# A new order of steps for an attention pair, with weight loads, x loads and one small addition moved

## The chip, the cores and the metric

The kernel runs on one core of a Trainium2 chip. The metric is the device time of one execution in microseconds. The engines meant below are TensorE (PE, with its weight loads PEld), VectorE (DVE), ScalarE (ACT), GpSimd (POOL) and SyncE (SP), whose queue issues nearly all transfers.

## The reference

Attention with a relative-position bias over 4 batches, 8 heads, 576 positions and head width 64, followed by a two-layer MLP with an ELU between its layers (2304 tokens, 512 to 2048 to 512):

```
scores = (q @ k.T) / 8 + bias          # bias: a small MLP of log1p(|i-j|) / log1p(i), per head
attn   = exp(scores - max); attn /= sum(attn) + 1e-9
x      = attn @ v, as 2304 x 512
h      = x @ w_in;  g = h if h > 0 else exp(h) - 1
out    = g @ w_out                     # the MLP's weights are given as float64
```

## The kernel before, in words

The program has three stages that follow each other: the bias is built (`bias_phase`), attention runs over 16 pairs of heads (`attention`), and the MLP (`mlp`) runs to the end. The order of instructions on every engine is that of the code; nothing reorders them.

**A pair.** Pair n (two heads of batch n // 4) has its scores in five groups: u = 0 to 3 are 128 query rows of both heads each, u = 4 holds the 64 rows that are left of both heads. A line of the table `STEPS` is one of the five steps 0 to 4 of an iteration; a token such as `aX20` has a prefix (`a`: the iteration's own pair n; `y`: the pair before it), a letter and numbers:

- `S u`: the score matmuls (`ps`, line 299). With u < 4 they fill two banks of PSUM, one for each head; there are two such buffers in all, so the next `S` waits until DVE has read them.
- `X u e`: `expo`. DVE adds the bias and takes the minimum (`ss<-ps,bias`, line 319), ACT takes exp (line 330), and after the second head GpSimd copies the last 64 columns to `md` (line 333).
- `T u`: PE transposes the result into two of three buffers `wt`; `P u r X` copies one of them to SBUF with engine A (ACT) or V (DVE). `M` and `Q` do the same for `md`; `M0a0` (`trans_spare`) uses spare columns of the score banks and needs two copies `Q`, `M0` (`trans_mid`) uses one of the three buffers and needs one.
- `V h j`: the matmuls with v (`wv`, line 426); half 0 takes u = 0, 1 and 4, half 1 takes u = 2 and 3. `C h X` copies a half out, from where SP stores it to `xd` in DRAM.

**The weights.** In iteration N the raw float64 weights of block f = N - 1 are turned into float32: `low` (GpSimd multiplies the upper words, line 273; DVE the lower words, line 277), `sign` (DVE, line 281; SP then issues the load of the next block's `raw`, which has a single buffer), `shift` (DVE, line 283, and then GpSimd's integer addition, line 286). SP stores the result to `wf` in iteration N + 1, after step 1.

**q and k.** `load_pair(n + 2)` issues five transfers; `high` (in step 2 of iteration N, DVE, line 118) and `rest` (in step 3, GpSimd, line 122: `kl`, `ql`, `qd`) split pair N + 1 into a high and a low part.

**x.** The table `early` gives a token (`one`, `two`) or the end of a step of iteration N something of the MLP's input: `load_x` (lines 466 and 470: 3 or 9 transfers of attention's output and of its reciprocal sums), `scale_x` (DVE multiplies them, line 478), `high_x` (line 501) and `low_x` (line 504).

**The sums.** After a batch's fourth pair `invert` adds 1e-9 (line 341) and takes the reciprocal (line 342), both by DVE, and `turn` transposes it for DRAM. After the last pair the lines of `LAST` are run, and then the MLP starts.

Of the kernel before, what the change touches and what calls it, by code (L numbers as in the profile page):

```python
# [24 lines left out]
def kernel(  # L25
# [68 lines left out]
    def load_pair(n):  # L94
        b, hp = pairs[n]
        kk, qq = st["kq", n] = [ld.tile([P, S], F32, tag=t, name=t, bufs=2) for t in ("kk", "qq")]

        nc.sync.dma_start(out=kk[0:D], in_=kT[b, hp, :, 0])
        nc.sync.dma_start(out=kk[D:P, 0:NCH * P], in_=kT[b, hp, :, 1, TAIL:])
        nc.sync.dma_start(out=kk[D:P, NCH * P:], in_=kT[b, hp, :, 1, 0:TAIL])  # L100
        for e in range(2):
            nc.sync.dma_start(out=qq[e * D:(e + 1) * D], in_=qT[b, hp, :, e])
# [21 lines left out]
    def load_v(n):  # L124
        b, hp = pairs[n]
        vv = st["v", n] = ld.tile([P, NU, D], F32, tag="vv", name="vv", bufs=2)
        nc.sync.dma_start(out=vv, in_=vt[b, hp])
# [210 lines left out]

    def invert(b):
        sm = st["sm", b].rearrange("p h u -> p (h u)")  # L340
        nc.vector.tensor_scalar(sm, sm, 1e-9, None, op0=ALU.add)
        nc.vector.reciprocal(sm, sm)

    def turn(b):
        sm = st.pop(("sm", b)).rearrange("p h u -> p (h u)")
# [182 lines left out]
    def attention():  # L528
# [6 lines left out]


        STEPS = (
# [5 lines left out]
        )  # L543
        LATE = (
# [5 lines left out]
        )  # L550
        LAST = (
            "yT3 yP30A yV00 yP31V yV01 yV02 yT2 yP20A yV03 yP21V yM0 yQ0V yM1 yQ1A",
            "yV04 yC0V yV10 yV11 yV12 yV13 yV14 yC1A",
        )
        late = []

        V, G = nc.vector, nc.gpsimd
        early = {
            (5, 1): [(load_x, 0, 0, 0)],
            (6, "one"): [(scale_x, 0, 0, 0, V)],  # L560
            (6, 1): [(load_x, 0, 1, 0)],
            (7, "one"): [(scale_x, 0, 1, 0, V)],
            (9, 1): [(load_x, 0, 0, 1)],
            (10, "one"): [(scale_x, 0, 0, 1, V)],
            (10, 1): [(load_x, 0, 1, 1)],
            (11, "one"): [(scale_x, 0, 1, 1, V)],
            (12, "two"): [(high_x, 0, "B11", xo["B11"], V.tensor_copy)],
            (13, "one"): [(low_x, 0, "B11", xo["B11"], V)],
            (13, "two"): [(high_x, 0, "B12", xo["B12"], V.tensor_copy)],
# [8 lines left out]
        def weights(f, op):  # L578
            if not 0 <= f < NFC:
                return  # L580
            if op == "low":
                decode(dp, f, "scale")
            decode(dp, f, op)
            if op == "sign" and f + 1 < NFC:
                decode(dp, f + 1, "load")
            if op == "shift":
                decode(dp, f, "add")
# [50 lines left out]
        def others(n, i):  # L638
            for fn, *args in early.get((n, i), ()):
                fn(*args)  # L640

        def aside(n, i):
            if i == 1:
                weights(n - 2, "store")
            if n == 0 and i == 2:
                split_high(1)
                split_low(1)
            if n > 0 and n % HP == 0:
                if i == 1:
                    invert(n // HP - 1)  # L650
                if i == 3:
                    late.extend(turn(n // HP - 1))
            others(n, i)
            if n < NP - 1:
                return
            if i == 0:
                load_w(0)
                load_w(1)
            if i == 2:
                high_w(0)  # L660
            if i == 3:
                low_w(0, nc.vector)
            if i == 4:
                load_w(2)
                high_w(1)

        for n in range(NP):
            for i, line in enumerate(STEPS if n < NP - 4 else LATE):
                flush()
                if i == 0:  # L670
                    if n + 2 < NP:
                        load_pair(n + 2)
                    load_v(n)
                step(n, line)
                aside(n, i)
        flush()
        weights(NP - 2, "store")
        weights(NP - 1, "low")
        weights(NP - 1, "sign")
        weights(NP - 1, "shift")  # L680
        invert(B - 1)
        others(NP, 0)
        step(NP, LAST[0])
        late += turn(B - 1)
        step(NP, LAST[1])
        weights(NP - 1, "store")
        others(NP, 1)
        low_w(1, nc.vector)
        flush()
        load_w(3)  # L690
        high_w(2)
# [351 lines left out]
```

## Time and profile before

| | us |
|---|---|
| median of 3 runs | 690.03 (688.99 to 690.52) |
| the profiled execution | 692.81 |
| its span, first to last instruction | 691.0 |
| PE, DVE, ACT, POOL busy in the span | 659.6, 483.8, 450.7, 133.7 |
| from the first score matmul of pair 0 to the MLP's first matmul | 56.4 to 306.9 |

The span is 1.8 us shorter than the profiled execution, and that execution is 2.8 us longer than the median of the runs. Times of rows count from the start of the span. The score matmuls of pair n's step 0 are where iteration n begins: pair 2 begins at 86.36 us, pair 15 at 283.63 us. PE's busy time is close to the whole span; its matmuls overlap, so the start of one instruction after another is the better measure of what they take.

### The profile page before, as it was taken

What the parts mean: (1) busy time and instruction counts of PE and PEld (TensorE: products, weight loads), DVE (VectorE), ACT (ScalarE), POOL (GpSimd) and SP (SyncE); (2) the same over time, 40 slices, a digit from 0 to 9 for tenths busy, and PEclk for the clock granted to TensorE, in tenths of its full rate; (3) what the DMA queues carried; (4) which work ended last, traced back from release to release, by engine and by line L of the source; (5) the groups of instructions that cost most, each with busy time, mean ns of one, the idle gap of its engine ahead of it and who ended that gap; (6) DMA issues with size and microseconds to landing.
All of it is one profiled execution on the core that took longest, in us unless ns stands there. A gap on an engine that the chain in (4) does not pass through costs nothing.

```text
span 691.0 us, 13847 instructions
## 1 busy us (share of the span) xinstructions
PE 659.6 (95%) x5246; PEld 528.1 (76%) x5246; DVE 483.8 (70%) x1003; ACT 450.7 (65%) x981; POOL 133.7 (19%) x168
## 2 busy tenths in 40 slices
PE   5997999979996999989999999999999999999997
PEld 3545667756675666769998898899899899899896
DVE  6997778858866798888777989745456754444443
ACT  6996789868885888967566666643444644344333
POOL 0002456545553555540000000000000000000000
PEclk9998899999998999999999999999999999999999
DMA  6999456776767556654678768998664465555202
GB/s 156 215 220 238 147 174 180 222 230 192 222 186 212 173 174 185 223 184 169 228 256 316 273 237 315 348 354 304 195 257 167 168 240 219 210 205 201 83 1 91
DMA packets 49938, 144.63 MB, mean 209 GB/s; under 512 B 13376, under 2 KB 26448, under 8 KB 42192
## 3 DMA queue, kind: packets, MB, share of 16 engines
q1 hardware_dynamic: 47840, 141.08, 63.0%
q10 hardware_dynamic: 2032, 2.67, 1.1%
q8 instruction: 41, 0.67, 0.4%
q14 instruction: 25, 0.20, 0.1%
HBM read 92.14 MB, written 40.97 MB: 193 GB/s over the span
## 4 chain that ended last, share of the span: by engine, by line
PE 72%; DMA 12%; ACT 8%; DVE 4%; issue 2%; SPq 1%; POOL 1%; DVEq 0%; ACTq 0%
PE acc L787 28%; PE h L836 26%; PE wv L426 7%; PE ps L299 6%; DMA raw<-in_wd_dram 4%; PE wt L384 3%; DMA wf<-da 3%; ACT bo L222 2%; ACT rel L199 2%; DMA bias<-bo 2%; DVE ss L319 2%; DMA rr<-rd 1%; ACT ss L330 1%; PE bps L209 1%; DMA T<-in_rtab_dram 1%
## 5 line engine op out<-in xcount | busy, mean ns | idle before, releaser
L787 PE MATMUL acc<-wB,gh 128*128 128x512 f32 x528 | 171.3, 392 | 0.0
L330 ACT ACTIVATE ss<-ss,nm 128x576 f32<-128x576 f32 x128 | 99.2, 778 | 26.7 <-DVE nm L319 26.3
L836 PE MATMUL h<-bias 128*128 128x384 f32 x552 | 111.4, 338 | 0.0
L787 PEld LDWEIGHTS acc<-wB,gh 128*128 128x128 f32 x528 | 98.1, 188 | 14.3
L319 DVE CUSTOM_DVE_ANT_0 ss<-ps,bias 128x576 f32<-128x576 f32 x128 | 91.6, 752 | 23.6 <-PE ps L299 12.1
L836 PEld LDWEIGHTS h<-bias 128*128 128x128 f32 x552 | 99.8, 188 | 7.5 <-DVE bias L504 0.4
L787 PE MATMUL acc<-wB,gl 128*128 128x512 f32 x264 | 103.8, 393 | 0.0
L816 ACT CAST gh<-e 128x384 fp32r<-128x384 f32 x96 | 49.4, 514 | 38.7 <-DVE e L815 37.7
L821 ACT ACTIVATE e<-c 128x384 f32<-128x384 f32 x66 | 34.6, 525 | 53.5 <-DVE c L867 53.4
L299 PE MATMUL ps<-kh,qh 64*128 64x288 f32 x256 | 52.2, 350 | 15.0 <-DVE nm L319 14.2
L810 DVE TENSOR_TENSOR gl<-e,gh 128x384 fp32r<-128x384 f32 x96 | 53.2, 554 | 18.9 <-ACT gh L816 16.4
L821 ACT ACTIVATE e<-h 128x384 f32<-128x384 f32 x28 | 13.8, 491 | 69.4 <-PE h L836 69.4
L815 DVE SCALAR_TENSOR_TENSOR e<-e,c 128x384 f32<-128x384 f32 x66 | 36.7, 557 | 30.6 <-ACT e L822 30.5
L299 PEld LDWEIGHTS ps<-kh,qh 64*128 64x128 f32 x256 | 29.8, 191 | 36.6 <-DVE nm L319 29.5
L836 PE MATMUL h<-bias,wA 128*128 128x384 f32 x276 | 56.3, 338 | 0.0
L426 PE MATMUL wv<-pta,vv 128*64 128x320 f32 (+1 forms) x320 | 55.6, 461 | 0.2 <-DVE pta L361 0.2
L209 PE MATMUL bps<-rel,cs 128*32 128x288 f32 x576 | 47.7, 424 | 8.2 <-ACT rel L199 7.8
L787 PEld LDWEIGHTS acc<-wB,gl 128*128 128x128 f32 x264 | 49.5, 187 | 7.8
L384 PEld LDWEIGHTS wt<-ident,ss 64*128 64x128 f32 x1024 | 44.6, 144 | 12.8 <-issue 6.2
L836 PEld LDWEIGHTS h<-bias,wA 128*128 128x128 f32 x276 | 50.2, 188 | 3.8
L384 PE MATMUL wt<-ident,ss 64*128 64x64 f32 x1024 | 50.0, 232 | 2.9 <-ACT ss L330 1.6
L822 ACT ACTIVATE e<-e 128x384 f32<-128x384 f32 x96 | 50.5, 526 | 3.0
(127 smaller groups left out, 1194.2 us busy)
## 6 DMA issues: line engine op xcount, KB each, us to landing
wB<-wB SPq DMA_DIRECT2D x22, 1024.0 KB, 5.0
raw<-in_wd_dram SPq DMA_DIRECT2D x16, 1024.0 KB, 6.9
bias<-wA SPq DMA_DIRECT2D x9, 1792.0 KB, 9.5
wA<-wA SPq DMA_DIRECT2D x8, 1792.0 KB, 12.0
wa<-wf SPq DMA_DIRECT2D x20, 512.0 KB, 5.0
bias<-bo SPq DMA_DIRECT2D x16, 576.0 KB, 8.4
wA<-bias SPq DMA_DIRECT2D x5, 1792.0 KB, 14.4
wf<-da SPq DMA_DIRECT2D x16, 512.0 KB, 8.2
```

The lines of the kernel that those rows point to most:

```text
L209: nc.tensor.matmul(ps[32 * g:32 * g + 32, f, 0:HS], lhsT=W2, rhs=rel[g][:, f * HS:(f + 1) * HS], start=True, stop=True,)
L299: nc.tensor.matmul(ps[:, f, 0:HS], lhsT=(qh, ql)[q][r, u * P:(u + 1) * P] if u < NCH else qd[n % 2][q], rhs=k[r, f * HS:(f + 1) * HS], sta ...
L319: nc.vector.tensor_tensor_reduce(out=s.rearrange("p (f x) -> p f x", f=2), in0=st["ps", n, u][e][:, :, 0:HS], in1=bap.rearrange("p (f x) - ...
L330: nc.scalar.activation(s, s, AF.Exp, bias=nm, scale=-1.0, accum_out=st["sm", b][:, hp, col:col + 1])
L384: nc.tensor.transpose(banks[r][:, x * TAIL:(x + 1) * TAIL], ss[q, c:c + P], ident[q, q])
L426: nc.tensor.matmul(st["pv", n, half][e * D:(e + 1) * D, 0:N], lhsT=l, rhs=r, start=start, stop=stop)
L787: nc.tensor.matmul(acc[j, t], lhsT=x[:, t * P:(t + 1) * P], rhs=w, start=(count[j, t] == 1), stop=(count[j, t] == 6 * NQ),)
L810: nc.vector.tensor_sub(gl, t, gh.bitcast(F32))
L816: nc.scalar.copy(g[i, e][0][:, h * HB:(h + 1) * HB], t)
L821: nc.scalar.activation(t, src, AF.Relu, scale=-1.0)
L822: nc.scalar.activation(t, t, AF.Exp, scale=-1.0)
L836: nc.tensor.matmul(ps, lhsT=a[f][c], rhs=x[y][c], start=(start and k == 0), stop=(stop and k == len(todo) - 1), skip_group_check=not start,)
```

## The change

`STEPS` and `LATE` (which have the same lines) get another order. `low` and `sign`, which stood on either side of `aX00` and `aX01`, follow each other on DVE; `shift` goes from step 1 to step 4. `trans_spare` is no longer used. The copies `P11` and `Q1` go from DVE to ACT, `C1` from ACT to DVE. `one` and `two` stand in step 3. `load_pair(n + 2)` is issued after step 2 and `load_v(n)` after step 0; both stood ahead of step 0. In `early` the loads of x get longer leads: from 1 to about 1.4 iterations for those of (5, 1) and (9, 1), and 2 iterations for the other two. The addition of 1e-9 becomes `lift` on GpSimd, after step 0; the reciprocal stays after step 1. `LAST` gets an order of its own, with the last block's weights inside.

```diff
     def invert(b):
         sm = st["sm", b].rearrange("p h u -> p (h u)")
-        nc.vector.tensor_scalar(sm, sm, 1e-9, None, op0=ALU.add)
         nc.vector.reciprocal(sm, sm)
+
+    def lift(b):
+        sm = st["sm", b].rearrange("p h u -> p (h u)")
+        nc.gpsimd.tensor_scalar(sm, sm, 1.0, 1e-9, op0=ALU.mult, op1=ALU.add)
...
         STEPS = (
-            "aS0 yM0a0 yT3 yQ01A yV02 one low aX00 yQ00A yP30A aX01 yV01 yV03",
...
+            "aS0 yT2 aX00 yP20A yP21A aX01 yV03 yV00 low",
+            "aS1 yT3 yV01 yP30A sign yV02 yM0 yP31A aX10",
+            "aS4 yQ0A aX11 yM1 yV04 yC0A yQ1A high aX40 aT0",
+            "aS2 two aP00A aP01A yV12 yV11 one yV14 aT4 rest aX20 aP40A aX21 aP41A",
+            "aS3 aT1 yV13 yV10 shift aP11A aP10A aX30 aX31 yC1V",
         )
...
         LAST = (
-            "yT3 yP30A yV00 yP31V yV01 yV02 yT2 yP20A yV03 yP21V yM0 yQ0V yM1 yQ1A",
-            "yV04 yC0V yV10 yV11 yV12 yV13 yV14 yC1A",
+            "yT2 yP20A yP21V yV00 yV01 low",
+            "yV02 yT3 yP30A yV03 yM0 yP31V yQ0V sign yM1 yQ1A",
+            "yV04 yC0V yV10 shift yV11 yV12 yV13 yV14 yC1A",
         )
...
             (5, 1): [(load_x, 0, 0, 0)],
-            (6, "one"): [(scale_x, 0, 0, 0, V)],
-            (6, 1): [(load_x, 0, 1, 0)],
-            (7, "one"): [(scale_x, 0, 1, 0, V)],
+            (6, "two"): [(scale_x, 0, 0, 0, V)],
+            (6, 3): [(load_x, 0, 1, 0)],
+            (8, "one"): [(scale_x, 0, 1, 0, V)],
             (9, 1): [(load_x, 0, 0, 1)],
-            (10, "one"): [(scale_x, 0, 0, 1, V)],
-            (10, 1): [(load_x, 0, 1, 1)],
-            (11, "one"): [(scale_x, 0, 1, 1, V)],
+            (10, "two"): [(scale_x, 0, 0, 1, V)],
+            (10, 3): [(load_x, 0, 1, 1)],
+            (12, "one"): [(scale_x, 0, 1, 1, V)],
...
         def aside(n, i):
             if i == 1:
                 weights(n - 2, "store")
+            if i == 0:
+                load_v(n)
+            if i == 2:
+                if n + 2 < NP:
+                    load_pair(n + 2)
...
             if n > 0 and n % HP == 0:
+                if i == 0:
+                    lift(n // HP - 1)
                 if i == 1:
                     invert(n // HP - 1)
...
                 flush()
-                if i == 0:
-                    if n + 2 < NP:
-                        load_pair(n + 2)
-                    load_v(n)
                 step(n, line)
                 aside(n, i)
         flush()
         weights(NP - 2, "store")
-        weights(NP - 1, "low")
-        weights(NP - 1, "sign")
-        weights(NP - 1, "shift")
+        lift(B - 1)
+        step(NP, LAST[0])
         invert(B - 1)
+        step(NP, LAST[1])
         others(NP, 0)
-        step(NP, LAST[0])
         late += turn(B - 1)
-        step(NP, LAST[1])
-        weights(NP - 1, "store")
+        step(NP, LAST[2])
         others(NP, 1)
         low_w(1, nc.vector)
+        weights(NP - 1, "store")
         flush()
```

Line numbers from 343 on are 3 higher in the changed kernel, and from 653 on a few more.

On SP, in iteration 9, where nine transfers for x are issued (`xr` and `rr`; `xd` and `wf` are stores), before:

```order
L439 DMA xd_75<-xs 128x256
L98 DMA kk<-in_k_dram 64x576
L99 DMA kk<-in_k_dram 64x512
L100 DMA kk<-in_k_dram 64x64
L102 DMA qq<-in_q_dram 64x576 x2
L127 DMA vv<-in_v_dram 128x576
L268 DMA raw<-in_wd_dram 128x2048
L288 DMA wf_89<-da 128x1024
L466 DMA xr_2302<-xd_74 128x2x128
L470 DMA rr<-rd_78 64x2x128 x2
L466 DMA xr_2302<-xd_74 128x2x64
```

and in the changed kernel:

```order
L442 DMA xd_75<-xs 128x256
L127 DMA vv<-in_v_dram 128x576
L268 DMA raw<-in_wd_dram 128x2048
L288 DMA wf_89<-da 128x1024
L469 DMA xr_2274<-xd_74 128x2x128
L473 DMA rr<-rd_78 64x2x128 x2
L469 DMA xr_2274<-xd_74 128x2x64
L473 DMA rr<-rd_78 64x2x64 x2
L469 DMA xr_2274<-xd_75 128x2x192
L473 DMA rr<-rd_79 64x2x192 x2
L98 DMA kk<-in_k_dram 64x576
```

The raw weights' load now has one transfer of v ahead of it in the iteration, not five of q and k as well; these come behind the loads of x.

On DVE, in steps 2 and 3 of iteration 13 (`high_x` is the cast of line 501 or 504, `low_x` the subtraction of line 504 or 507; the casts of line 118 are `high`), before:

```order
L319 ISA st_116,nm<-ps,biast 128x576
L319 ISA nm 128x1
L501 CAST bias<-xr_2302 128x768
L118 CAST qd_111<-qq 64x64 x2
L118 CAST qh<-qq 128x512
L118 CAST kh<-kk 128x576
L319 ISA ss,nm<-ps,bias 128x576
L319 ISA nm 128x1
L319 ISA ss,nm<-ps,bias 128x576
L319 ISA nm 128x1
L403 COPY pta<-wt 128x8x64
```

and in the changed kernel:

```order
L118 CAST qd_111<-qq 64x64 x2
L118 CAST qh<-qq 128x512
L118 CAST kh<-kk 128x576
L319 ISA st_116,nm<-ps,biast 128x576
L319 ISA nm 128x1
L504 CAST bias<-xr_2274 128x768
L507 TENSOR_TENSOR bias<-xr_2274,bias 128x768
L319 ISA ss,nm<-ps,bias 128x576
L319 ISA nm 128x1
L319 ISA ss,nm<-ps,bias 128x576
L319 ISA nm 128x1
L283 TENSOR_SCALAR da<-da 128x1024
```

`high` now stands ahead of `aX40`, and both operations on x stand between it and `aX20`, behind `high`, whose last cast lets GpSimd begin `rest`.

On GpSimd, around the change of batch after pair 11, in the changed kernel:

```order
L122 TENSOR_TENSOR kl<-kk,kh 128x576
L122 TENSOR_TENSOR ql<-qq,qh 128x512
L122 TENSOR_TENSOR qd_112<-qq,qd_111 64x64 x2
L333 TENSOR_SCALAR md<-ss 128x128
L286 TENSOR_TENSOR da<-da,dm 128x1024
L333 TENSOR_SCALAR md<-ss 128x128 x2
L273 TENSOR_SCALAR da<-raw 128x1024
L345 TENSOR_SCALAR sm<-sm 128x36
L333 TENSOR_SCALAR md<-ss 128x128
```

The addition of line 286 now stands between the copies `md` of u = 2 and u = 3, and line 345 is the new `lift`.

## Rows read from the trace of the kernel before

**Rows 1.** Busy time by stretch: PE, PEld, DVE, ACT, POOL, granted clock, DMA.

```profile
70.18:86.36 16.18, 16.09 (x174) 11.37 (x174) 11.72 (x30) 13.43 (x37) 7.97 (x10) 0.84 0.46 142
86.36:283.63 197.27, 184.37 (x2267) 129.49 (x2265) 154.51 (x370) 164.55 (x430) 107.33 (x130) 0.97 0.66 197
190.97:204.47 13.50, 13.50 (x177) 9.57 (x175) 10.91 (x27) 12.68 (x34) 7.96 (x10) 1.00 0.62 188
141.95:161.38 19.43, 15.42 (x176) 10.72 (x174) 11.77 (x28) 12.73 (x34) 7.88 (x10) 0.91 0.76 217
204.47:225.94 21.47, 16.21 (x176) 11.62 (x174) 11.86 (x28) 12.72 (x34) 7.95 (x10) 0.84 0.73 207
...
175.76:190.97 15.21, 14.55 (x178) 10.06 (x177) 12.92 (x31) 12.62 (x34) 8.21 (x10) 1.00 0.65 193
...
306.87:684.40 377.53, 377.53 (x1875) 340.44 (x1874) 237.45 (x420) 195.79 (x377) 1.37 (x1) 1.00 0.59 218
```

**Rows 2.** Timeline of DVE at the two long stalls: start, duration, idle before.

```profile
146.55 0.96 DVE L478 TENSOR_TENSOR xr<-xr,rr 128x768 f32<-128x768 f32 x1 [4.69 <-DMA rr<-rd]
...
210.31 0.96 DVE L478 TENSOR_TENSOR xr<-xr,rr 128x768 f32<-128x768 f32 x1 [5.93 <-DMA xd<-xs]
```

**Rows 3.** Waits: total us, times, longest.

```profile
DVE dm L277 <- DMA raw<-in_wd_dram: 5.3, 4, 2.0
```

**Rows 4.** Timeline of PE, steps 0 to 2 of pair 9.

```profile
190.97 0.40 PE L299 MATMUL ps<-kh,qh 64*128 64x288 f32 x2
...
191.86 0.28 PE L369 MATMUL ps<-ident,md 64*128 64x64 f32 x4
191.98 0.78 PE L384 MATMUL wt<-ident,ss 64*128 64x64 f32 x16
192.69 1.84 PE L426 MATMUL wv<-pta,vv 128*64 128x320 f32 x12
194.46 0.40 PE L299 MATMUL ps<-kh,qh 64*128 64x288 f32 x2
...
196.63 0.44 PE L358 MATMUL wm<-ident,md 128*128 128x128 f32 x2
```

**Rows 5.** Timeline of DVE after the scores of pair 9's step 0.

```profile
192.28 0.76 DVE L319 CUSTOM_DVE_ANT_0 ss<-ps,bias 128x576 f32<-128x576 f32 x1 [0.80 <-PE ps L369]
...
193.64 1.22 DVE L281 SCALAR_TENSOR_TENSOR dm<-raw,dm 128x1024 uint32<-128x1024 uint32 x1
```

**Rows 6.** Timeline of ACT: a copy `P` of pair 9.

```profile
195.25 0.58 ACT L403 COPY ptb<-wt 128x512 f32<-128x512 f32 x1
```

**Rows 7.** Timeline of DVE: the addition of 1e-9 twice, and `low_x` after the last pair.

```profile
120.24 1.22 DVE L341 TENSOR_SCALAR sm<-sm 128x36 f32<-128x36 f32 x1
...
301.42 0.18 DVE L341 TENSOR_SCALAR sm<-sm 128x36 f32<-128x36 f32 x1
...
304.94 1.60 DVE L504 TENSOR_TENSOR bias<-xr,bias 128x768 fp32r<-128x768 f32 x1
```

**Rows 8.** Timeline of POOL beside these, and `rest` of pair 8.

```profile
119.03 2.38 POOL L286 TENSOR_TENSOR da<-da,dm 128x1024 int32<-128x1024 int32 x1
...
186.53 1.42 POOL L122 TENSOR_TENSOR kl<-kk,kh 128x576 fp32r<-128x576 f32 x1 [1.85 <-DVE kh L118]
187.89 1.30 POOL L122 TENSOR_TENSOR ql<-qq,qh 128x512 fp32r<-128x512 f32 x1
...
303.90 1.82 POOL L492 TENSOR_TENSOR xr<-xr 128x768 f32<-128x768 f32 x1
```

**Rows 9.** Groups of DVE from 56 to 312 us: busy us, mean ns.

```profile
L501 DVE CAST bias<-xr 128x768 fp32r<-128x768 f32 x4 | 2.2, 554 | 0.0
```

**Rows 10.** Transfers of `raw`, us from issue to landing, all 16.

```profile
DMA to landing us min/median/max: 5.7/6.9/9.5
```

**Rows 11.** Timeline of SP: when pair 9's `raw` is issued.

```profile
197.88 0.36 SPq L268 DMA_DIRECT2D raw<-in_wd_dram  x1
```

**Rows 12.** Timeline of PE at the end of attention.

```profile
298.52 0.46 PE L384 MATMUL wt<-ident,ss 64*128 64x64 f32 x8 [1.29 <-ACT ss L330]
```

14 rows, old and new, of tables (LATE, STEPS) are left out of this document.

## The prediction

> **What bounds the kernel now.** I read the busy time by stretch first, then the timelines of the stretches that stand out. From 306.87 us on, PE is busy for the whole of 377.53 us at full clock [rows 1]: the MLP can only begin earlier or later. The change acts between 56 and 307 us, and the measure is the distance from one pair's first score matmul to the next one's.
>
> Pair 9 takes 13.50 us, and PE is busy in all of it [rows 1]: a pair without a wait. The 13 pairs 2 to 14 take 197.27 us, where 13 such pairs would take 13 x 13.50 = 175.5. So 21.8 us are waits. Pair 6 takes 19.43 and pair 10 takes 21.47 us, 5.9 and 8.0 too much, and both have one cause: DVE multiplies x as `one` in step 0, ahead of the pair's first `X`, and stood idle for 4.69 and 5.93 us until that transfer landed [rows 2]. PE, whose score banks DVE empties, stood behind it and was granted 0.91 and 0.84 of its clock over these pairs; pair 9 had all of it [rows 1]. Pair 8, in which a batch's sums are inverted, takes 15.21, 1.7 too much; pairs 4 and 12 are of its kind. DVE also waited for raw weights, 5.3 us in 4 pairs [rows 3].
>
> **PE's own work.** Nothing is removed from it. The spare-bank transposes `M0a0` become `M0`: 4 small matmuls that hold PE for 0.12 us (191.86 to 191.98) become two of the kind that lasts 0.44 and not 0.28 us [rows 4]; +0.1 a pair. The order moves PE's fill between scores. Step 0 had 3.49 us (190.97 to 194.46). Now it has scores 0.89, transposes 0.71 and two thirds of the value matmuls' 1.77, together 2.78 [rows 4]. DVE starts its first `X` 1.31 us after the scores begin and is through the second at 2.67, when `sign` starts [rows 4, 5]; with a tenth for the signal the next scores can start at about 2.8. PE and DVE are level there, where there was 0.7 us of slack, so I charge 0.15 a pair for jitter. `low` and `sign` then run beside the scores of step 1, whose fill has grown to 2.1 us. A pair without a wait: 13.50 + 0.1 + 0.15 = 13.75, x 13 = 178.8.
>
> ACT gains a copy of 0.58 us (`P11`) [rows 6] and `Q1` and loses `C1`, of like width; `Q0` becomes one copy from two. That adds 0.3 to 0.6 to the 12.68 of 13.50 us that it is busy [rows 1]: 13.0 to 13.3 of 13.75, and so still under PE.
>
> **Loads of x.** `scale_x` moves from step 0 to step 3, about 8 us later for the loads of (5, 1) and (9, 1); the waits were 4.69 and 5.93 us [rows 2]. The other two get over a pair more. I cost what remains at nothing. SP issues the nine transfers behind `raw`, and behind them stand only q and k, which DVE needs a pair later.
>
> **The small addition.** It took 1.22 us at 120.24 and 0.18 at 301.42, for the same 36 columns [rows 7]. The first ended at 121.46, just behind GpSimd's integer addition at 121.41 (119.03 + 2.38) [rows 8]: it was held until the other engine was done. On GpSimd it costs DVE nothing; the reciprocal stays. The transposition of the sums stays too, and the reciprocal now pushes `X11`, `high` and `X40`: I leave 0.5 in each of pairs 4, 8 and 12, 1.5 together.
>
> **What the new place of `one` and `two` costs.** The same hold works against the change. `high` now ends before `X40`, so GpSimd's `rest` begins while DVE is in `X40`: `kl` 1.42, `ql` 1.30 us [rows 8]. DVE then comes to a cast of 0.55 (`two`) [rows 9] and an operation of 0.96 (`one`) [rows 2], ahead of `X20`. Alone they take 1.5 us, and `X20` must wait as long anyway: 0.2 until its scores begin and 1.31 from there. Beside GpSimd they need not: after the last pair `low_x`, of the size of the 0.96, took 1.60 from 304.94 on, ending 0.82 behind GpSimd's subtraction at 305.72 (303.90 + 1.82) [rows 7, 8]. In pairs 12, 13 and 14 both stand there with `rest` (pair 15 has no `rest`; pairs 6, 8 and 10 have one operation). If `kl` comes first, DVE waits some 1.2 us for it, does the cast, waits 1.30 for `ql`, does the other: 4.0, which is 2.5 too late. If DVE's cast comes first, it waits for `kl` once: 0.55 + 1.42 + 0.96 = 2.9, or 1.4 too late. PE has about 0.15 of slack before step 3, so 1.25 to 2.35 in each of the three pairs. A single operation costs 0 to 0.6. Together 3.8 to 8.9; which comes first hangs on 0.2 us that my placing cannot resolve, so I take the middle, 6.3.
>
> The Trainium skill, page "SBUF — State Buffer", section "Who interferes with whom", says the same of the mechanism: GpSimd shares a port pair with VectorE, a VectorE instruction with two SBUF inputs or in a two-port mode competes for it, and the one that starts second "fully blocks". The 1.22 us bear that out. If it were a sharing by bandwidth instead, by the 1.60 against 0.96 us, the 1.5 us would become 2.5 and cost 0.85 in three pairs, 2.6 in all, and the time would be 3.7 lower than by the block.
>
> **Raw weights.** Landing took them 5.7 to 9.5 us [rows 10]. Their load waited on SP behind five transfers of q and k: pair 9's went out at 197.88 [rows 11], 3 us after `sign`, which ran from 193.64 for 1.22 [rows 5]. Now it goes out when `sign` and GpSimd's multiplication are done. The latter stands behind an `md` that needs ACT's exp, which I place 6 us into the pair. `low` wants the data 2.8 us into the next one, 10.5 us later. So the 5.3 us go.
>
> **Start and end.** Pair 1 (16.18 us at a granted clock of 0.84 [rows 1]) keeps its work and its cause, a pair 0 with no older pair to fill PE: 0, between -1.5 and +1.5. At the end PE waited 1.29 us for an exp [rows 12] and a little more behind it, since `T3` came first. Now `T2` does, whose exp is older. `Q0` on DVE gives back 0.3. I take -1.3, between -2 and 0. GpSimd's subtractions for the MLP now precede its last integer addition; their users come 4 us or more into the MLP.
>
> **The sum.** 178.8 + 1.5 + 6.3 = 186.6 against 197.3 is -10.7; with the end -12.0. From the profiled execution's 692.81 that is 680.8. The runs' median is 2.78 below that execution, which I carry over: 678.0 us.
>
> **Rivals.**
> 1. *The hold does not bite*, because GpSimd starts `rest` later than I place it, behind DVE's work on x. Then the 6.3 us vanish: 671.7. For it: `rest` also stands behind an `md` that waits for ACT. Against it: it began within 0.1 us of the last cast at 186.53 [rows 8].
> 2. *ACT becomes the bound.* Busy for 13.0 to 13.3 us, it also waits in each pair for a last value matmul before `C0` and for `T4` before `P40`, some 0.7 us as I place them. If these add up, a pair takes 14.0 to 14.2, about 0.35 more than 13.75: +4.5, so 682.5. Against it: it waited about 0.8 per pair before (13.50 - 12.68) and PE was full all the same [rows 1].
> 3. *Slower: GpSimd's integer addition catches `low`.* `shift` now sits in step 4, and the addition of 2.38 us [rows 8] behind it and behind an `md`. I place its end 1.6 us into the next pair, 1.2 us ahead of `low`. If ACT runs over 1.2 us later than I think, `low` is held as the small addition was, for up to 2.38, and `sign` and `X10` with it; 0.5 of that is slack. At 1.9 x 13 = 24.7 us the time is 702.7. It is slower than before once a pair loses 0.9 (12.0 / 13). Against it: ACT would have to fall that far behind in every pair.
> 4. *The change does not do what it says*: transfers queue as before and x or `raw` is waited for at the new places. Half of the 13.9 us of pairs 6 and 10 stays, 7.0: 685.0. Against it: 8 us of lead against waits of 5.93 at most.
>
> **Chances.** The forecast, 674 to 681.5: 0.52. Rival 1: 0.20. Rival 2: 0.13. Rival 4: 0.09. Rival 3: 0.06. The range 670.5 to 685.5 takes in the first four mostly and both ends of the hold's price. Anything within 0.2% of before (1.4 us, about what a measurement of this kernel can tell from no change) could only lie between rivals 3 and 4: faster 0.92, same 0.02, slower 0.06.
>
> **What would show it.** In the trace of the changed kernel: pairs 6 and 10 within 1 us of pair 9, and the multiplication of x with no idle time before it; no idle time before `low`; pairs 3, 5, 7, 9 and 11 at 13.6 to 13.9; pairs 12 to 14 at 15 to 16.5, with DVE's two operations between `X40` and `X20` longer than 0.55 and 0.96 and ending just behind a subtraction of GpSimd; the reciprocal without a long wait; `T2` at the end without idle time. I am wrong if ordinary pairs take over 14.2, or if pairs 12 to 14 look like pair 11.

## The result and the profile after

The changed kernel takes 679.0 us, the median of 4 runs (677.5 to 680.9), beside 690.0 us for the kernel before (689.0 to 690.5): a ratio of 0.984, with a 95% interval of 0.982 to 0.987. The forecast was 678.0. Its profiled execution took 678.97 us with a span of 677.1, where the one before had 692.81 and 691.0.

The forecast total was nearly met, but not by its own terms; in part that was luck. The busy time by stretch shows it; the columns are those of [rows 1]. The rows are, in order: pair 1; pairs 2 to 14; pair 9; pairs 4, 10, 12 and 13; pair 15 with the end of attention; the MLP.

```profile
69.93:85.54 15.61, 15.54 (x174) 10.95 (x172) 10.70 (x26) 13.53 (x35) 6.16 (x10) 0.86 0.45 136
85.54:268.82 183.28, 179.26 (x2241) 126.06 (x2239) 147.86 (x354) 167.93 (x431) 113.49 (x134) 1.00 0.72 211
183.56:197.12 13.56, 13.56 (x174) 9.58 (x172) 10.35 (x27) 12.55 (x34) 8.04 (x11) 1.00 0.60 178
112.64:127.75 15.11, 14.29 (x175) 9.93 (x173) 10.86 (x29) 13.37 (x35) 8.48 (x12) 1.00 0.71 210
197.12:211.88 14.76, 14.06 (x174) 9.89 (x172) 11.94 (x29) 13.11 (x35) 9.07 (x11) 1.00 0.83 248
225.36:241.81 16.45, 14.76 (x175) 10.11 (x174) 14.04 (x32) 13.02 (x35) 9.26 (x12) 1.00 0.74 239
241.81:255.26 13.45, 13.45 (x175) 9.49 (x173) 12.42 (x29) 12.79 (x34) 9.26 (x11) 1.00 0.58 175
268.82:290.82 22.00, 21.66 (x251) 13.81 (x249) 18.43 (x37) 18.02 (x44) 12.19 (x12) 1.00 0.64 204
290.82:677.10 386.28, 380.83 (x1886) 342.25 (x1884) 241.62 (x424) 197.47 (x380) 3.61 (x2) 1.00 0.59 219
```

Pairs 2 to 14 went from 197.27 [rows 1] to 183.28: -14.0, where -10.7 was forecast. Pair 15 and the end went from 23.24 to 22.00 (-1.2). What lies before pair 2 lost 0.8. The MLP, costed at nothing, went from 384.1 (306.87 to the end at 691.0) to 386.28: +2.15. Together that is -13.9, the difference of the spans. The long stalls of pairs 6 and 10 are gone, and with them the lowered clock: pairs 2 to 14 are granted 1.00, where [rows 1] had 0.97.

Three new waits stand in the trace. **The first** is in pairs 4, 8 and 12: the reciprocal waits 1.26 us for GpSimd's small addition. The timelines are POOL, then DVE, then PE, in pair 4; the columns are start, duration, the instruction, and in brackets the idle time before it and what ended it.

```profile
117.38 0.30 POOL L333 TENSOR_SCALAR md<-ss 128x128 f32<-128x128 f32 x1 [2.28 <-ACT ss L330]
117.64 1.18 POOL L273 TENSOR_SCALAR da<-raw 128x1024 f32<-128x1024 f32 x1
118.90 0.22 POOL L345 TENSOR_SCALAR sm<-sm 128x36 f32<-128x36 f32 x1
...
119.15 0.38 DVE L341 RECIPROCAL sm<-sm 128x36 f32<-128x36 f32 x1 [1.26 <-POOL sm L345]
119.45 0.70 DVE L319 CUSTOM_DVE_ANT_0 ss<-ps,bias 128x576 f32<-128x576 f32 x1
...
122.01 0.39 PE L299 MATMUL ps<-kh,qh 64*128 64x288 f32 x1 [0.82 <-DVE nm L319]
```

The addition itself is 0.22 us. But it is issued behind step 0, and so it stands in GpSimd's order behind an `md` that waits for ACT and behind the conversion of the raw weights. DVE, in its own order, has the reciprocal ahead of `X11`, and PE then waits 0.82 us for the score bank that `X11` should have emptied. Read such a wait from the queue of the engine that is named: the instruction named is short, what stands ahead of it is not.

**The second** is the hold between GpSimd and DVE, which was forecast for pairs 12 to 14. It is there in pair 12 and absent in pair 13. DVE and POOL, pair 12 and then pair 13:

```profile
234.61 1.36 DVE L504 CAST bias<-xr 128x768 fp32r<-128x768 f32 x1
235.89 2.02 DVE L481 TENSOR_TENSOR xr<-xr,rr 128x768 f32<-128x768 f32 x1
...
234.14 1.41 POOL L122 TENSOR_TENSOR kl<-kk,kh 128x576 fp32r<-128x576 f32 x1
235.52 1.58 POOL L122 TENSOR_TENSOR ql<-qq,qh 128x512 fp32r<-128x512 f32 x1
...
249.45 0.55 DVE L504 CAST bias<-xr 128x768 fp32r<-128x768 f32 x1
249.92 0.94 DVE L507 TENSOR_TENSOR bias<-xr,bias 128x768 fp32r<-128x768 f32 x1
...
249.24 0.30 POOL L333 TENSOR_SCALAR md<-ss 128x128 f32<-128x128 f32 x1 [1.34 <-ACT ss L330]
249.50 2.65 POOL L122 TENSOR_TENSOR kl<-kk,kh 128x576 fp32r<-128x576 f32 x1
```

In pair 12 `kl` is 0.47 us ahead of the cast: the cast takes 1.36 instead of 0.55, and the multiplication behind it, held by `ql`, 2.02 instead of 0.96. In pair 13 the cast is 0.05 us ahead: DVE does both at full speed, and `kl` takes 2.65 instead of 1.42. Pair 14 is like pair 13. In both, `kl` stands behind an `md` that waits for ACT. Why `kl` comes first in pair 12 is argued and not shown: there alone of the three DVE has a reciprocal to do ahead of `X11`, and where that waits for nothing (lift_first, below) `kl` is still 0.36 us ahead. GpSimd has time to spare there (9.26 of 13.45 us busy).

**The third** is in the MLP: PE waits 1.37 us for the ELU. POOL, DVE, the DMA queue of SP, and PE at its start:

```profile
292.02 3.04 POOL L286 TENSOR_TENSOR da<-da,dm 128x1024 int32<-128x1024 int32 x1 [0.63 <-DVE da L283]
...
292.73 3.41 DVE L518 TENSOR_TENSOR bias<-wa,bias 128x1024 fp32r<-128x1024 f32 x1
298.14 0.96 DVE L495 TENSOR_TENSOR T<-xr,xr 128x768 f32<-128x768 f32 x1 [0.87 <-DMA rd<-rs]
...
295.08 0.32 SPq L288 DMA_DIRECT2D wf<-da  x1
295.50 0.35 SPq L353 DMA_DIRECT2D rd<-rs  x1
...
309.62 0.62 PE L842 MATMUL h<-bias 128*128 128x384 f32 x2 [1.37 <-DVE e L821]
```

GpSimd's last integer addition now runs beside the MLP's weights subtraction (`low_w`), which takes 3.41 us instead of 1.2 and ends 1.1 behind the addition. The same addition holds up the last store of the weights on SP, and behind that store stands `rd<-rs`, for which `T` waits another 0.87. All of DVE's work at the MLP's start is late, and the ELU stands behind it.

Two forecasts are borne out. DVE no longer waits for raw weights (5.3 us in [rows 3], none now), and the multiplication of x has no idle time in front of it. In pair 10 the wait has changed its place: q now comes late, by 1.49 us.

```profile
204.55 0.42 DVE L118 CAST qd<-qq 64x64 fp32r<-64x64 f32 x2 [1.49 <-DMA qq<-in_q_dram]
```

Its loads were issued on SP only from 198.32 on, behind the nine transfers of x that went out from 190.64 to 198.3.

### The profile page after: what moved, and what is told of

Same layout as the page of the kernel before. It is cut to its first block, busy times and chain, and to the rows that moved or that the text cites. A ratio compares the mean times of both kernels' runs of the same rounds, so it can differ in the third digit from the quotient of the medians.

```text
span 677.1 us, 13812 instructions
## 1 busy us (share of the span) xinstructions
PE 654.4 (97%) x5216; PEld 524.4 (77%) x5216; DVE 477.3 (70%) x983; ACT 454.3 (67%) x982; POOL 140.9 (21%) x172
## 4 chain that ended last, share of the span: by engine, by line
PE 82%; ACT 7%; DMA 4%; DVE 4%; issue 2%; POOL 0%; SPq 0%; DVEq 0%; ACTq 0%; POOLq 0%
PE acc L793 28%; PE h L842 25%; PE wv L429 11%; PE ps L299 10%; PE wt L387 4%; ACT rel L199 3%; ACT bo L222 3%; DMA wa<-wf 1%; DMA xd<-xs 1%; DVE ss L319 1%; PE wm L361 1%; DMA bias<-bo 1%; PE wt L395 1%; DMA T<-in_rtab_dram 1%; PE bps L209 1%
## 5 line engine op out<-in xcount | busy, mean ns | idle before, releaser
L299 PE MATMUL ps<-kh,qh 64*128 64x288 f32 x256 | 54.3, 347 | 6.2 <-DVE nm L319 5.5
L209 PE MATMUL bps<-rel,cs 128*32 128x288 f32 x576 | 46.0, 431 | 9.9 <-ACT rel L199 7.8
L429 PE MATMUL wv<-pta,vv 128*64 128x320 f32 (+1 forms) x320 | 54.1, 450 | 0.2 <-DVE pta L364 0.2
L873 DVE TENSOR_TENSOR c<-h,u 128x384 f32<-128x384 f32 x66 | 36.6, 555 | 20.1 <-PE h L842 20.1
L299 PEld LDWEIGHTS ps<-kh,qh 64*128 64x128 f32 x256 | 32.6, 191 | 22.6 <-DVE nm L319 15.1
```

Of the source, the lines that this page charges most:

```text
L209: nc.tensor.matmul(ps[32 * g:32 * g + 32, f, 0:HS], lhsT=W2, rhs=rel[g][:, f * HS:(f + 1) * HS], start=True, stop=True,)
L299: nc.tensor.matmul(ps[:, f, 0:HS], lhsT=(qh, ql)[q][r, u * P:(u + 1) * P] if u < NCH else qd[n % 2][q], rhs=k[r, f * HS:(f + 1) * HS], sta ...
L429: nc.tensor.matmul(st["pv", n, half][e * D:(e + 1) * D, 0:N], lhsT=l, rhs=r, start=start, stop=stop)
```

## The experiments

All twelve were timed beside the kernel before, on three occasions on which its median was 691.2, 692.8 and 693.2 us, so the ratios are what can be compared. The changed kernel itself was timed on an occasion before these, at 0.984, and differences of a few tenths of a per cent from it prove little. Where stretches are compared, they are those of one profiled execution each. Pair 1 differs by 1.5 us between executions whose instructions up to there are the same (15.6 us at a clock of 0.86 above, 14.06 at 1.00 in others), so I go by pairs 2 to 14, the end and the MLP.

**x_leads_only**: the kernel before, with only the changed table of x loads and uses.

```
-            (6, "one"): [(scale_x, 0, 0, 0, V)],
+            (6, "two"): [(scale_x, 0, 0, 0, V)],
...
```

> The kernel before, with only the longer leads of the x loads (the table of early work); steps, load order of q, k, v and the small addition stay. Theory A (the two long stalls were the whole of the loss): pairs 6 and 10, 19.4 and 21.5 us before, fall to 13.5 to 14.5, pairs 4, 8 and 12 stay at 14.2, 15.2 and 15.3, and the profiled time falls by 12 to 14 us of the 13.8 that the full change brought, median 677 to 679. Rival B (the new order of steps is needed as well, since raw weights and the sums still stop DVE): it falls by only 7 to 10 us, median 680 to 683.

Measured: 681.8 us, ratio 0.987 (0.983 to 0.991); pairs 2 to 14 take 186.51. Pairs 6 and 10 fell to 13.84 each, so the leads alone cure them. But raw weights were now waited for 10.3 us in 6 pairs, where it was 5.3 in 4 [rows 3]:

```profile
216.22 0.69 DVE L277 TENSOR_SCALAR dm<-raw 128x1024 int32<-128x1024 uint32 x1 [3.91 <-DMA raw<-in_wd_dram]
```

The two pairs gave back 13.2 us, and the other eleven took 2.5 us more. The time is the second theory's, but not its reason: the next run shows that the order of the loads is what was lacking, and not the new order of steps.

**x_and_raw**: that, and the order of the loads of raw, v, q and k from the change. Steps, addition and end stay as they were.

```
-                if i == 0:
-                    if n + 2 < NP:
-                        load_pair(n + 2)
-                    load_v(n)
...
+            if i == 0:
+                load_v(n)
+            if i == 2:
+                if n + 2 < NP:
+                    load_pair(n + 2)
```

> The kernel before with two parts of the change: the longer leads of the x loads, and q, k and v issued behind the raw weights; steps, sums and last lines stay. Theory A (with the leads alone DVE still waited 10.3 us for raw weights; ahead of q and k they come in time): DVE waits less than 3 us for raw weights, pairs 3, 5, 7, 9 and 11 take 13.5 to 13.8, pairs 4, 8 and 12 keep the small addition on DVE (14 to 14.3 in 4 and 8), median 673 to 676, so 6 to 8 below the leads alone. Rival B (the raw weights come late by the transfers of x, and not by q and k): at least 6 us of waits stay and the median is 679 or more.

Measured: 675.9 us, ratio 0.974 (0.971 to 0.977). Pairs 2 to 14 take 179.77, the MLP 384.2. One wait for raw weights is left, 1.6 us in pair 12. The first theory holds. The two edits on the loads bring more than the whole change, whose interval (0.982 to 0.987) lies wholly above this one. By the ratios the rest of the change costs about 1%; by the stretches from pair 2 on it costs 4.4 us, or 0.65%: 3.5 in the pairs and 2.1 in the MLP, less the 1.2 that the end gains.

**old_steps**: the changed kernel, with the order of the steps taken back. **lift_first**: the changed kernel, with the small addition issued ahead of step 0.

```
-            "aS0 yT2 aX00 yP20A yP21A aX01 yV03 yV00 low",
+            "aS0 yM0a0 yT3 yQ01A yV02 one low aX00 yQ00A yP30A aX01 yV01 yV03",
...
```

```
                 flush()
+                if i == 0 and n > 0 and n % HP == 0:
+                    lift(n // HP - 1)
                 step(n, line)
...
-                if i == 0:
-                    lift(n // HP - 1)
```

> The changed kernel with the old lines of steps 0 to 4, everything else as changed (longer x leads, q and k behind the raw weights, the addition on GpSimd, the new last lines). Theory A (the order of steps moves little by itself, since an ordinary pair took 13.50 and takes 13.55): 677 to 680, the same as the changed kernel within 0.3%; pairs 4, 8 and 12 lose the wait of the reciprocal or keep it, by where GpSimd's multiplication stands. Rival B (the order carries a third of the gain): 682 to 685.

> The changed kernel with the small addition on GpSimd issued at the head of step 0 and not behind it, so that it stands ahead of GpSimd's multiplication of the raw weights. Theory A (the reciprocal waited 1.26 us because the addition stood behind a copy that waits for exp and behind the 1.18 us multiplication): no wait before the reciprocal; pairs 4 and 8 go from 15.1 to 13.9 (13.55, the transposition of the sums and the reciprocal), pair 12 from 16.45 to 14.0 to 15.4 (to 14.0 if DVE now comes to its two operations before GpSimd's first subtraction, as in pairs 13 and 14); the profiled span is 3.4 to 5 us shorter, median about 675. Rival B (these pairs are long because the reciprocal itself pushes the chain X11, casts, X40): they stay at 14.8 or more and the time is within 1 us of the changed kernel's.

old_steps: 672.8 us, ratio 0.975 (0.971 to 0.980), better than either theory had it: the new order of the steps carries no gain, it costs 4.7 us. Ordinary pairs take 13.45 to 13.50, pairs 4 and 8 13.70, and pairs 2 to 14 178.55, beside 183.28. With the old order GpSimd's addition is out before the reciprocal of pairs 4 and 8 needs it, and of DVE's operations on x in pairs 6 to 15 only one cast is held (0.83 us instead of 0.55, in pair 12). Pair 12 takes 15.45, with a wait of 1.8 us for raw weights. The MLP still takes 386.1, so that loss doesn't come from the steps. It comes with the new end: the two kernels with the old one, x_leads_only and x_and_raw, have 384.2.

lift_first: 675.0 us, ratio 0.977 (0.974 to 0.981). Pairs 4 and 8 fell from 15.1 to 13.90, as the first theory said, pair 12 from 16.45 to 15.56, where it had 15.4 at most. DVE and POOL in pair 4:

```profile
116.17 0.38 DVE L341 RECIPROCAL sm<-sm 128x36 f32<-128x36 f32 x1
...
113.54 0.22 POOL L345 TENSOR_SCALAR sm<-sm 128x36 f32<-128x36 f32 x1
```

The addition is out 2.4 us before the reciprocal, and nothing waits. This prices the first wait: 1.2 us in pairs 4 and 8 each. In pair 12 it brings 0.9, for there a wait of 0.26 us for raw weights, at 225.87, takes its place in part. So the changed kernel has no wait for raw weights in part, it seems, because it is late itself. Pair 10 was longer here (16.14), with q 2.9 us late, which hides part of the gain.

**rest_first**: the changed kernel, with the copy `md` of the second spare tile moved behind `rest`, so that GpSimd begins `kl` earlier.

```
-        if u < NCH and e == 1:
+        if u < NCH and e == 1 and not (u == 1 and 0 < n < NP - 1):
...
+                        if tok == "rest":
+                            tail(N, 1)
```

> The changed kernel with GpSimd's copy of u = 1 issued behind the subtractions that split q and k (for pairs 1 to 14), so that the first subtraction starts when the casts end and before DVE reaches its operations on x. Theory A (an exclusive hold, and whoever starts first has it): in pairs 13 and 14 the cast waits for the first subtraction; if DVE's two operations follow without letting GpSimd in, each pair loses 0.7 to 1.3 us, if GpSimd's second subtraction gets in between, 2.0 to 2.5; pairs 6 and 8 lose 0 to 0.6. Together 2 to 6 us slower than the changed kernel. Rival B (the two share bandwidth): the operations of 0.55 and 0.94 us take 0.9 and 1.6, pairs 13 and 14 lose 0.9 each at most, and it is less than 2 us slower. Rival C (no contention: pairs 10 and 12 were long for other reasons): no change.

Measured: 682.7 us, ratio 0.990 (0.985 to 0.995). Pairs 13 and 14 rose from 13.45 and 13.57 to 14.90 and 14.88. DVE and POOL in pair 13:

```profile
251.08 1.38 DVE L507 CAST bias<-xr 128x768 fp32r<-128x768 f32 x1
252.38 2.03 DVE L510 TENSOR_TENSOR bias<-xr,bias 128x768 fp32r<-128x768 f32 x1
...
250.62 1.42 POOL L122 TENSOR_TENSOR kl<-kk,kh 128x576 fp32r<-128x576 f32 x1 [1.10 <-PE ps L299]
252.00 1.59 POOL L122 TENSOR_TENSOR ql<-qq,qh 128x512 fp32r<-128x512 f32 x1
```

With `kl` 0.46 us ahead, DVE's two operations take 3.3 instead of 1.4 us, and the pair pays 1.45 (pair 14 1.3). The first theory holds in kind. Of its two cases it is the second, since `ql` gets in between DVE's two operations, but its price of 2.0 to 2.5 was too high. So the block that the prediction forecast is there, and GpSimd's two subtractions both hold DVE, as it placed them. But its price for `kl` first was 2.35, and 1.3 to 1.45 came: in pair 13 the two operations took 3.3 us from the start of one to the end of the other, and not the 4.0 that it added up. The other half of the loss is pair 10 (17.75), where q came 3.1 us late; why that varies (1.5, 2.9 and 3.1 us in three kernels with the same order of loads) stays open.

**x_behind_q**: the changed kernel, with the x load of pair 9 behind the loads of q and k.

```
-            (9, 1): [(load_x, 0, 0, 1)],
+            (9, 2): [(load_x, 0, 0, 1)],
```

> The changed kernel, with the nine transfers of x of iteration 9 issued after step 2 and so behind the loads of q and k. Theory A (pair 10 took 14.8 us because q was landed 1.5 us late behind these transfers, and DVE's multiplication of x then fell behind GpSimd's first subtraction): no wait for q, and pair 10 takes 13.5 to 13.9; 0.9 to 1.3 us shorter in the profile, 677.5 to 678.5 as a median, which is within what a measurement can tell. Rival B (pair 10 is long by the hold between DVE and GpSimd alone): it stays at 14.2 or more.

Measured: 676.9 us, ratio 0.977 (0.974 to 0.980). Pair 10 fell from 14.76 to 13.91, with no idle time before q's cast, although x's multiplication there is still held (2.11 instead of 0.96 us). The first theory holds for this pair. So of pair 10's 1.2 us over an ordinary pair, 0.85 is the queue and 0.35 the hold.

**add_on_dve**: the changed kernel, with 1e-9 added by DVE again.

```
+        nc.vector.tensor_scalar(sm, sm, 1e-9, None, op0=ALU.add)
         nc.vector.reciprocal(sm, sm)
```

> The changed kernel with one edit taken back: 1e-9 is added by VectorE again, in front of the reciprocal, and GpSimd's small addition is gone. In the changed kernel the reciprocal of pairs 4, 8 and 12 starts 1.3 us late, behind GpSimd's subtraction and conversion. Theory A (what holds it there is GpSimd's conversion of the weights, whoever adds: VectorE's small addition comes up while the conversion runs and is stretched until it ends): pairs 4 and 8 stay at 15.0 to 15.2 us, the small addition takes about 1.2 us instead of 0.18, and the whole stays within 0.3% of the changed kernel (ratio to the kernel before 0.977 to 0.985). Theory B (the move to GpSimd itself costs the time, since the addition stands behind the conversion in GpSimd's order): VectorE adds in 0.2 us, pairs 4 and 8 fall to 13.7 to 13.9, ratio about 3.5 us (0.005) better than the changed kernel's.

Measured: 679.6 us, ratio 0.980 (0.977 to 0.983). Pair 4 takes 14.87 us, 0.24 less than with GpSimd. The addition is held until GpSimd's conversion ends at 118.38:

```profile
117.35 1.06 DVE L341 TENSOR_SCALAR sm<-sm 128x36 f32<-128x36 f32 x1
118.45 0.38 DVE L342 RECIPROCAL sm<-sm 128x36 f32<-128x36 f32 x1
...
117.19 1.19 POOL L273 TENSOR_SCALAR da<-raw 128x1024 f32<-128x1024 f32 x1
```

The first theory holds, a little beyond its range for pair 4: in this order of steps DVE meets the conversion either way, and moving the addition changed the wait's name and made it 0.2 us worse. So what costs the time is the place of the small operation beside the conversion, and not the engine that does it.

**late_shift**: the changed kernel, with the last integer addition issued behind DVE's weights subtraction. **old_steps_late_shift**: the same on old_steps, with the x loads of pairs 6 and 10 one step earlier.

```
-            "yV04 yC0V yV10 shift yV11 yV12 yV13 yV14 yC1A",
+            "yV04 yC0V yV10 yV11 yV12 yV13 yV14 yC1A",
...
         low_w(1, nc.vector)
+        weights(NP - 1, "shift")
         weights(NP - 1, "store")
```

> The changed kernel, with the last block's shift (and so GpSimd's last integer addition) issued behind low_w(1) and not inside the last line. Theory A (the MLP lost about 2 us because the addition, which starts as DVE comes to low_w(1), holds it for 3 us and with it the MLP's first ELU): low_w(1) takes 1.2 and not 3.4 us, no wait of a product for an ELU of line 821, and from the MLP's first matmul to the end 384.1 to 384.6 us where the changed kernel has 386.3; median about 677. Rival B (the MLP is late for its weights' loads): the wait stays and the time too.

> The changed kernel with the old lines of steps 0 to 4 (which alone gave 672.8), the last shift behind low_w(1), and the second and fourth load of x after step 2, not 3, of iterations 6 and 10. Theory A: the MLP gets back 1.5 to 2 us, and the 1.8 us for which DVE waited for raw weights in pair 12 go or shrink; 669 to 671. Rival B (both were hidden, or the old order pays elsewhere): 672 to 674.

late_shift: 683.2 us, ratio 0.984 (0.981 to 0.988), no gain; neither theory holds. The subtraction is free now (1.21 us each), yet the MLP takes 388.5, longer than with the addition early. DVE, POOL and the DMA queue of SP:

```profile
293.00 1.21 DVE L518 TENSOR_TENSOR bias<-wa,bias 128x1024 fp32r<-128x1024 f32 x1
299.55 0.96 DVE L495 TENSOR_TENSOR T<-xr,xr 128x768 f32<-128x768 f32 x1 [5.34 <-DMA rd<-rs]
...
293.15 3.31 POOL L286 TENSOR_TENSOR da<-da,dm 128x1024 int32<-128x1024 int32 x1 [2.63 <-DVE da L283]
...
296.49 0.32 SPq L288 DMA_DIRECT2D wf<-da  x1
296.90 0.35 SPq L353 DMA_DIRECT2D rd<-rs  x1
```

Counted from the MLP's first matmul (289.94 here, 290.82 in the changed kernel), the addition starts 2.0 us later, the store that waits for it goes out 2.3 us later, and `rd` and `T` behind it as well. By about as much, 2.24 us, the MLP is longer. My reading of the MLP's loss as a held subtraction left out the larger part, the queue. old_steps_late_shift: 674.0 us, ratio 0.974 (0.970 to 0.979). Pairs 2 to 14 take 176.85, the MLP 388.3: what the loads gave, the end took back. The wait for raw weights in pair 12 is gone, as the first theory had it; the time is the second's.

**rd_first**: the changed kernel, with the last attention stores issued ahead of the last weights store.

```
         low_w(1, nc.vector)
+        flush()
         weights(NP - 1, "store")
-        flush()
```

> The changed kernel with one edit: at the end of the attention part the store of the reciprocals and of the attention output are issued on SyncE's queue ahead of the last store of the weights, not behind it. Theory A (T2 in the MLP waits for the read of the reciprocals' tile, which stands on the queue behind the weights' store, which waits for GpSimd's last integer addition; VectorE's weights subtraction is held by the same addition and sets the next limit): the wait of 0.9 us in front of T2 goes, PE's wait at the MLP's start falls from 1.4 to 0.4-0.7 us, the MLP takes 385.2 to 385.7 instead of 386.3. Theory B (only VectorE's held subtraction sets the MLP's start): the MLP stays at 386.2 to 386.5.

Measured: 677.0 us, ratio 0.978 (0.975 to 0.982). The MLP takes 384.76, 1.5 less; PE's wait fell from 1.37 to 0.35. DVE and SP:

```profile
290.93 4.55 DVE L518 TENSOR_TENSOR bias<-wa,bias 128x1024 fp32r<-128x1024 f32 x2
295.40 0.95 DVE L495 TENSOR_TENSOR T<-xr,xr 128x768 f32<-128x768 f32 x1
...
288.13 0.31 SPq L353 DMA_DIRECT2D rd<-rs  x1
293.28 0.32 SPq L288 DMA_DIRECT2D wf<-da  x1
```

The subtraction is held as before, but `T` follows it at once. So 1.5 of the 2.15 us were the order of the stores on one queue. The held subtraction may be the rest, 0.6; no run takes it away by itself. It gained more than the first theory said.

**new_cured**: the changed kernel with all four cures together (lift_first, x load behind q, late shift, rd_first). **old_cured**: the old order of steps with three of them; the x load of pair 9 stays ahead of q and k, and those of pairs 6 and 10 are issued one step earlier than in the changed kernel.

> The changed kernel's order of steps with the four cures together: small addition ahead of step 0 of pairs 4, 8, 12; the x load of pair 9 behind the q and k loads; the weights' last integer addition behind VectorE's last subtraction; the last stores in the order reciprocals first. Theory A (the stalls found are additive: two of 1.2 us in pairs 4 and 8, 0.9 in pair 12, 0.7 in pair 10, and the MLP back at 384.2): pairs 4 and 8 at 13.9, pairs 2 to 14 in 178.5 to 179.5 us, the MLP at 384.1 to 384.5, span 668.5 to 670.5, ratio 0.969 to 0.974. Theory B (removing one stall brings the next, as when the shift was put late): MLP above 385.5 or pairs 2 to 14 above 181, span over 672.

> The order of steps of the kernel before, with the early x loads and the raw weights ahead of q and k of the changed kernel, the small addition on GpSimd ahead of step 0, the last integer addition behind VectorE's last subtraction, and the reciprocals stored first at the end. Theory A (as above: pairs 2 to 14 at 176.5 to 177.2 us, the end at 21.6, the MLP at 384.1 to 384.5): span 666 to 667.5, ratio 0.966 to 0.971, and some 2.5 us under the new order with the same cures, which would then be the price of the new order itself. Theory B (the new order costs nothing once its stalls are cured): within 1 us of the other kernel of this call with all four cures.

new_cured: 679.1 us, ratio 0.980 (0.976 to 0.984); old_cured: 673.5 us, ratio 0.974 (0.970 to 0.978). In the pairs the cures add up as expected on the old order (176.65), and miss that by 0.3 us on the new (179.80). In the MLP they don't: 387.4 and 388.5, where 384.1 to 384.5 was expected, and for the whole time neither kernel's first theory holds. DVE and POOL of new_cured, in pair 12 (the first line) and at the MLP's start:

```profile
225.88 0.69 DVE L277 TENSOR_SCALAR dm<-raw 128x1024 int32<-128x1024 uint32 x1 [0.95 <-DMA raw<-in_wd_dram]
...
291.69 3.14 DVE L495 TENSOR_TENSOR T<-xr,xr 128x768 f32<-128x768 f32 x1
...
300.34 1.23 DVE L518 TENSOR_TENSOR bias<-wa,bias 128x1024 fp32r<-128x1024 f32 x1 [2.95 <-ACT bias L514]
...
290.71 3.31 POOL L286 TENSOR_TENSOR da<-da,dm 128x1024 int32<-128x1024 int32 x1 [2.63 <-DVE da L283]
```

The late addition now holds `T` (3.14 instead of 0.96 us), and the last store and the weights loads behind it are later still. The late shift was the wrong cure; rd_first without it wasn't tried on the old steps. Between their pairs 2 to 14 lie 3.15 us. Pair 12 has 2.56 of it (16.27 and 13.71). Of these, 0.95 is a wait for raw weights that old_cured does not have and that may come from the x loads, which stand elsewhere on the queue there; about 1.4 is the hold, for in the new order `kl` is first there. So the 3.15 us are not the price of the order of steps alone.

x_and_raw, old_steps, old_steps_late_shift and old_cured, at ratios of 0.974 to 0.975, beat the kernel before and, across occasions, the changed one, and can't be told apart. x_and_raw does it with two edits.

## Why the prediction was right, point by point

The time was 1.0 us off, but by errors that cancelled. Pairs 2 to 14 were forecast 3.3 us too long and the start 0.8; the MLP's 2.15, which the forecast did not have, took most of that away. So the profiled execution, forecast at 680.8, took 678.97, which is 1.8 less. The last term, 2.78 us from the profiled execution down to the median, then failed: in the changed kernel the two are the same, 678.97 and 679.0. That the median came within 1.0 us is luck in good part; the fall of the two long pairs, which is most of the gain, is not.

- **Ordinary pairs** at 13.75: 13.45 to 13.57, so 13 x 0.2 = 2.6 too much. The 0.15 for jitter was not there. PE and DVE came out level as placed (in pair 9 the scores of step 1 start 2.91 us after those of step 0, and DVE is through its second `X` at 2.73), and PE was full all the same (13.56 of 13.56).
- **The loads of x**: right but for pair 10. The two pairs came down by 5.9 and 6.7 us. x_leads_only shows that the leads do this alone; pair 10's remaining queue wait for q (0.85) was not costed. I had named the nine transfers ahead of q and k and called it enough that q is needed a pair later.
- **Raw weights**: right, though the changed kernel has little to spare (0.26 us of it came back in lift_first, 0.95 in new_cured). x_leads_only and x_and_raw show that the order of the loads, not the place of `low`, removes the wait: 10.3 us with the loads left alone, 1.6 with them moved and the steps left alone.
- **The small addition**: the step that failed. "On GpSimd it costs DVE nothing" left out what stands ahead of it on GpSimd. 1.5 us were forecast for the three pairs, 0.5 each for the reciprocal and the transposition. Pairs 4 and 8 lost 1.55 and 1.6: 0.35 for those two, as lift_first leaves it, and 1.2 for the wait. Pair 12 has the same wait of 1.26 us, so I put 1.55 there too: 4.7. Leaving the addition on DVE would have lost nearly as much (add_on_dve), so the term was wrong for the new order of steps, whoever adds.
- **The hold**: right in kind, mis-sized. 6.3 us were forecast for six pairs. Pair 12 lost 1.35 (16.45 - 13.55 - 1.55), pair 10 0.35, the rest nothing: 1.7. The case that the text called undecidable, on 0.2 us, fell one way in pair 12 and the other in pairs 13 and 14; there even the lower end of 1.25 did not apply, since DVE's second operation follows the first without a gap. I had let GpSimd in between them. Where `kl` is first, the forecast had 2.35, and pair 12 and rest_first have 1.3 to 1.45. So both ends were about 1 us too high. The Trainium skill, "SBUF — State Buffer", section "Who interferes with whom", has the later starter blocked, and the trace agrees in both directions: 0.55 became 1.36 us on DVE, 1.42 became 2.65 on GpSimd.
- Check of these: 13 x 13.55 + 4.7 + 1.7 + 0.85 = 183.4, and 183.28 was measured.
- **Start and end**: -1.3 forecast for the end, -1.2 found; 0 within 1.5 for the start, -0.8 found. The end belongs to the new last lines: 21.6 to 22.0 us with them in every run, 23.2 without. The 0.3 charged there for `Q0` on DVE had no ground, since the last lines had it on DVE before as well (`yQ0V`).
- **The MLP**: "their users come 4 us or more into the MLP" looked at GpSimd's subtractions, and not at what the integer addition behind them holds: DVE's subtraction, and the stores queued behind its result. +2.15, of which rd_first takes back 1.5. So the new end cost more than the 1.2 us that it gave.
- **Rivals**: the first (no hold) came true in pairs 13 and 14. ACT did not become the bound (12.55 of 13.56). The integer addition never caught `low` in the pairs; what it caught was the MLP's subtraction.
- **The signs**: ordinary pairs came out just under the 13.6 to 13.9 that was named. Pair 10 was 1.2 us over pair 9, not within 1, and the reciprocal had a wait. Of pairs 12 to 14 only pair 12 shows the hold as described; 13 and 14 look like pair 11 (13.45 and 13.57 beside 13.48), which the text itself had named as a sign of being wrong.

## What to carry to other kernels

When a small instruction is moved to another engine to spare the first one, write down what stands ahead of it in that engine's order at that moment; its own 0.2 us is not its price. The same holds for a DMA queue: a store that waits for its data holds every transfer issued behind it, and issuing the last attention stores ahead of one weights store gave 1.5 us. Time the parts of a compound change apart: here two edits on the load order carried the whole gain and more, and the reordering of the steps hid a loss of 4.7 us, 0.7%.

## What the runs showed of the hardware that was not expected

The block between DVE and GpSimd is not symmetric in who gets in between. Two DVE operations in a row (0.55 and 0.94 us) kept `kl` out for both, 2.65 us instead of 1.42. But DVE's held cast got in between GpSimd's `kl` and `ql`, which stand as close together: it ended 0.4 us behind `kl`, and `ql` was stretched from 1.28 to 1.58. A lead of 0.05 us was enough for DVE to go first, and only DVE's losses cost the kernel time. And an operation on 36 columns can be held as a large one is, for what is left of the other engine's operation: 0.18 us alone [rows 7], 1.06 beside the conversion.
